# Moving one ScalarE copy and one set of V loads to other places in the instruction order of an attention and feed-forward kernel

## Chip, cores, metric

One core of one Trainium2 chip. The metric is the device time of one execution in microseconds (us), median of several runs.

## The reference

Batch 8, 8 heads, sequence S = 576, head dimension D = 64. Heads 0 to 3 use a local mask, heads 4 to 7 a strided one. The attention output, viewed as 4608 tokens of 512, goes through a feed-forward layer with a leaky activation.

```python
scores = scale * np.matmul(q, k.transpose(0, 1, 3, 2))
mask_local   = (rel >= 0) & (rel < 32)
mask_strided = (rel >= 0) & (pos[None, :] % 32 == pos[:, None] % 32)
# heads 0..3 local, heads 4..7 strided; masked softmax over the last axis
x = (attn @ v).transpose(0, 2, 1, 3).reshape(B * S, H * D)
h = x @ w_in                                    # 512 -> 2048
out = (np.maximum(h, 0) + alpha * np.minimum(h, 0)) @ w_out
```

## The kernel before

Two things run interleaved: the feed-forward matmuls of a chunk of 512 tokens (`lin1_piece`, line 570, and `lin2_piece`, line 611) and the attention of the batch after it, cut into small pieces that are fed in between. Attention works in pairs of heads, four pairs to a batch: pairs 0 and 1 are local, 2 and 3 strided. From batch 2 on, three of the four results are transposed by a DMA through the crossbar. The result of the first strided pair needs one more reordering: ScalarE copies it from the landing tile `xs` into `xT`, the input of the feed-forward layer (line 435). The fourth pair is transposed on TensorE (`x_piece`).

```python
pspool = ctx.enter_context(tc.tile_pool(name="ps", bufs=3, space=bass.MemoryType.PSUM))
# ...
def load_v(b, strided):                 # local V: one of two buffers, vls[b % 2]; issued by GpSimd, casts
    # ...
    keep(nc.gpsimd.dma_start(v16[r0:128, :, 0:64], ...))     # 3072 rows of 64 elements
# ...
def score_both(P):                      # the scores of a pair, in two halves
    # half 0: PSUM "sp"; exp (L366) and mask on GpSimd (L368) at once
    # half 1: two PSUM tiles of pool "ps"; its two exps (L372) are deferred by a piece each
    defer.extend([lambda: ex(0), lambda: ex(1)])
# ...
def x_piece(P):
    xp = pspool.tile([128, 1024], F16, tag="ps", name="xp")  # needs a "ps" buffer: freed by ex(0)
    for t in range(P.n):
        keep(nc.tensor.transpose(xp[...], P.x16[...], ident[...]))              # L413
    # ... keep(nc.scalar.copy(xT[...], xp[...]))                                 # L417

def x_dma(P):
    P.xs = xpool.tile([128, 8, 80], F16, tag="xs", bufs=2, name="xs")
    keep(nc.sync.dma_start_transpose(P.xs, P.x16[0:80, :]))                     # L428

def x_copy(P):
    keep(nc.scalar.copy(xT[:, P.hp, base : base + S]..., P.xs[:, :, 0:72]...))  # L435
```

For step g the pieces are: scores of pair g (S), the probability-times-V pieces of pair g-1 (P), the TensorE transposes of queries and keys (T), those of the result of pair g-2 (X). Each piece may carry loads and copies:

```python
def run(...):
    fn()
    # ... casts of V, q and k
    if lastp:
        if 4 * DX <= g - 1 < npair and pairs[g - 1].xd:
            x_dma(pairs[g - 1])
        if g % 4 == 0 and DX <= c < B:
            transpose_d()
        if g % 4 == 2 and DX <= c and c + 1 < B:
            load_d(c + 1)               # strided q and k of the next batch (qsd, ksd)
        if g % 4 == 2 and c + 2 < B:
            load_v(c + 2, False)        # local V, two batches ahead
    if copyp and 4 * DX <= g - 2 < npair and pairs[g - 2].xd and pairs[g - 2].strided:
        x_copy(pairs[g - 2])
```

Here c = g // 4 is the batch. For batch 2 the pairs are 8 to 11: V of batch 4 and q and k of batch 3 are loaded in step 10, the DMA of pair 10 is issued in step 11, its copy in the third piece of step 12, and the transposes of pair 11 come in step 13.

The softmax here doesn't subtract the row's maximum and nothing guards it: scores larger than these inputs give would overflow.

## Time and profile before

| | before |
|---|---|
| median | 328.12 us (3 runs, 328.0 to 329.12) |
| span of the profiled run | 326.4 us |
| TensorE busy | 314.9 us |
| TensorE idle | 11.5 us, of which one wait of 4.02 us |
| landing of the xs DMA after its issue | 2.6 us least, 2.7 median, 8.4 most |

A wait line reads: engine, tile and line that waited, "<-", what it waited for, then total us, times, longest. In the lines in order of time the columns are start, duration, engine, line, what; in brackets stands the idle time of that engine before it and what ended it. The lines themselves are shown in the prediction.

### The profile page before, as it was taken

The page shows a single profiled execution, that of the slowest core. Times are in us where ns is not written, and L with a number is a line of the kernel's source. Part 1 is how long each engine was busy: PE and PEld are TensorE (multiplying, and loading weights), DVE is VectorE, ACT ScalarE, POOL GpSimd, SP SyncE. Part 2 cuts the span into 40 slices and gives each one's busy share as a digit, 9 for nine tenths or more (in the row PEclk, how much of TensorE's full clock was granted, in tenths as well). Part 3 has the DMA queues.
Part 4 walks back from the last instruction along what each step waited for, and adds up shares of the span by engine and source line. Part 5 has one row for each costly group of instructions (what it writes and reads, how often), then busy time and mean ns, then how long its engine had stood idle before and what let it go on. Part 6 is the DMA issues. An engine that isn't in the chain of part 4 may idle for free.

```text
span 326.4 us, 6321 instructions
## 1 busy us (share of the span) xinstructions
PE 314.9 (96%) x2493; PEld 162.9 (50%) x2493; DVE 182.4 (56%) x356; ACT 173.1 (53%) x321; POOL 140.8 (43%) x152
## 2 busy tenths in 40 slices
PE   7999999999995999999999999999999999999995
PEld 3564455554552445444558754445544444444444
DVE  5576836488540884278427843784378328505801
ACT  2655655477335664576457735773566247415610
POOL 8832397308996362936293619351803300000000
PEclk9999999999997999999999999999999999999999
DMA  7999999996499798969987997371710230021011
GB/s 220 192 206 206 226 225 176 146 252 172 91 152 149 198 113 89 171 192 104 97 127 237 104 85 147 91 92 40 160 50 1 58 91 22 0 93 38 0 64 64
DMA packets 77597, 40.33 MB, mean 124 GB/s; under 512 B 58480, under 2 KB 69248, under 8 KB 77568
## 3 DMA queue, kind: packets, MB, share of 16 engines
q0 software_dynamic: 41728, 17.38, 49.2%
q1 hardware_dynamic: 35840, 22.55, 28.0%
q8 instruction: 19, 0.31, 0.4%
q14 instruction: 10, 0.08, 0.1%
HBM read 38.01 MB, written 9.44 MB: 145 GB/s over the span
## 4 chain that ended last, share of the span: by engine, by line
PE 85%; issue 4%; DMA 4%; DVE 2%; POOL 2%; ACT 1%; SPq 0%; POOLq 0%; ACTq 0%; DVEq 0%
PE hps L570 35%; PE ops L611 34%; PE pv L396 4%; DMA xs<-x16s 3%; PE tp L235 2%; PE wps L633 2%; DMA ql<-in_q_dram 2%; PE sp L353 1%; PE ops L603 1%; PE xp L413 1%; PE sp L311 1%; PE sph L311 1%; PE sph L353 1%; DVE x L405 1%; DVE qT L177 1%
## 5 line engine op out<-in xcount | busy, mean ns | idle before, releaser
L583 DVE SCALAR_TENSOR_TENSOR gT<-neg,oma,hps 128x512 f16<-128x512 f32 x144 | 106.2, 744 | 57.3 <-ACT neg L580 49.3
L611 PE MATMUL ops<-wout,gT 128*128 128x512 f16 x560 | 135.7, 380 | 0.0
L570 PE MATMUL hps<-xT,win 128*128 128x512 f16 (+1 forms) x640 | 134.0, 360 | 0.4
L580 ACT ACTIVATE neg<-hps 128x512 f32<-128x512 f32 x144 | 86.0, 597 | 40.1 <-PE hps L570 40.1
L570 PEld LDWEIGHTS <-win 128*128 128x128 f16 x640 | 60.6, 98 | 60.7 <-issue 5.3
L611 PEld LDWEIGHTS <-gT 128*128 128x128 f16 x560 | 49.2, 98 | 47.2
L368 POOL TENSOR_TENSOR et<-et,consts 128x576 f16<-128x576 f16 (+1 forms) x24 | 30.6, 1273 | 89.3 <-ACT et L366 89.2
L616 ACT COPY osb<-ops 128x512 f32<-128x512 f32 x35 | 20.5, 585 | 57.3 <-PE ops L611 53.3
L403 DVE RECIPROCAL rc<-pv 72x6 f32<-72x6 f32 (+2 forms) x80 | 14.9, 186 | 53.2 <-PE pv L396 52.7
L405 DVE TENSOR_TENSOR x<-pv,rc 96x384 f16<-96x384 f32 (+2 forms) x62 | 33.0, 532 | 2.1
L396 PEld LDWEIGHTS <-et 72*128 72x128 f16 (+1 forms) x448 | 24.1, 98 | 16.6 <-POOL et L375 0.9
L375 POOL TENSOR_TENSOR et<-et,consts 128x576 f16<-128x576 f16 (+1 forms) x24 | 30.5, 1270 | 0.2 <-POOL et L368 0.2
L366 ACT ACTIVATE et<-sp 128x576 f16<-128x576 f32 (+1 forms) x24 | 15.5, 646 | 10.6 <-PE sp L353 10.6
L372 ACT ACTIVATE et<-sph 128x288 f16<-128x288 f32 (+1 forms) x48 | 18.6, 409 | 0.0
L633 PE MATMUL wps<-wrm 128*128 128x512 f16 x44 | 16.4, 449 | 1.2 <-DVE wrm L645 1.2
L396 PE MATMUL pv<-vs,et 72*128 72x65 f16 x256 | 15.7, 193 | 0.0
L167 POOL DMA_DIRECT2D vl<-in_v_dram x8 | 11.1, 1390 | 9.5 <-PE pv L396 7.8
L179 POOL COPY vs<-stv 72x1024 f16<-72x1024 f16 x14 | 14.4, 1035 | 0.0
L177 DVE COPY qT<-tp 128x1024 f16<-128x1024 f16 (+1 forms) x10 | 10.1, 1008 | 4.1 <-PE tp L235 4.1
L353 PEld LDWEIGHTS <-kT 64*128 64x128 f16 x336 | 7.1, 95 | 9.9 <-issue 8.9
L435 ACT COPY xT<-xs 128x576 f16<-128x576 f16 x6 | 7.8, 1308 | 7.6 <-DMA xs<-x16s 7.6
L417 ACT COPY xT<-xp 128x576 f16<-128x576 f16 x10 | 6.4, 639 | 10.1 <-PE xp L413 10.1
(79 smaller groups left out, 201.6 us busy)
## 6 DMA issues: line engine op xcount, KB each, us to landing
out_dram<-osb SPq DMA_DIRECT2D x35, 256.0 KB, 2.3
ql<-in_q_dram SPq DMA_DIRECT2D x6, 512.0 KB, 4.8
kl<-in_k_dram SPq DMA_DIRECT2D x6, 512.0 KB, 5.4
stv<-in_v_dram POOLq DMA_DIRECT2D x8, 288.0 KB, 6.7
vl<-in_v_dram POOLq DMA_DIRECT2D x6, 384.0 KB, 10.1
win<-in_moe_w_in_dram POOLq DMA_DIRECT2D x4, 512.0 KB, 9.4
wout<-in_moe_w_out_dram POOLq DMA_DIRECT2D x4, 512.0 KB, 17.0
qsd<-in_q_dram POOLq DMA_DIRECT2D x6, 288.0 KB, 7.0
```

What stands on the lines that cost most here:

```text
L366: keep(nc.scalar.activation(ev.rearrange("r (y c) -> r y c", y=2), sp[0:r, :, 0:n], AF.Exp, scale=SCALE))
L368: keep(nc.gpsimd.tensor_tensor(mv, mv, m, op=ALU.mult))
L372: keep(nc.scalar.activation(ev[:, n * y : n * y + n], sps[y][0:r, 0:n], AF.Exp, scale=SCALE))
L375: keep(nc.gpsimd.tensor_tensor(mv, mv, m, op=ALU.mult))
L396: keep(nc.tensor.matmul(pv[:, 65 * x : 65 * x + 65], et[0:r, c : c + 128], v16[0:r, 2 * P.pr + hh, t, :] if P.strided else v16[:, 6 * (2 * ...
L405: keep(nc.vector.tensor_tensor(P.x16[0:w, c0 : c0 + 64 * nb].rearrange("r (c e) -> r c e", e=64), pvv[:, :, 0:64], rc[0:w, 0:nb].unsqueeze ...
L570: keep(nc.tensor.matmul(hps[:, dst : dst + w], win16[:, kk, 128 * m : 128 * m + 128], xT[:, kk, src : src + w], start=(kk == 0 and x == 0) ...
L580: keep(nc.scalar.activation(neg, hps, AF.Relu, scale=-1.0))
L583: keep(nc.vector.scalar_tensor_tensor(gTs[n][:, m, :], neg, oma[:, m : m + 1], hps, op0=ALU.mult, op1=ALU.add))
L611: keep(nc.tensor.matmul(ops, gTs[n][:, kf, 128 * mt : 128 * mt + 128], wout16[:, kf, :], start=(kf == 0), stop=(kf == 15)))
L616: keep(nc.scalar.copy(osb, ops))
L633: keep(nc.tensor.matmul(wps, wrm[:, 0:128], wrm, start=True, stop=True))
```

## The change

Its intent: a copy on ScalarE that waits for a DMA holds up what is behind it in ScalarE's queue (in the trace before, all of it ran only after the copy, from 100.50 us on). The copy is placed one step later, so that the DMA has landed by then, and the local V loads of batches 4 to 7, of which that of batch 4 was in flight together with this DMA, are issued three steps later (V of batch 4 in step 13 instead of 10).

```diff
-        copyP = min(2, len(seq) - 1)
...
-                    if g % 4 == 2 and c + 2 < B:
-                        load_v(c + 2, False)
-                if copyp and 4 * DX <= g - 2 < npair and pairs[g - 2].xd and pairs[g - 2].strided:
-                    x_copy(pairs[g - 2])
+                    if g % 4 == 1 and DX < c and c + 1 < B:
+                        load_v(c + 1, False)
+                if first and 4 * DX <= g - 3 < npair and pairs[g - 3].xd and pairs[g - 3].strided:
+                    x_copy(pairs[g - 3])
```

(`first` is the first piece of a step. The lines after it move up by one: L570, L611, L616 become L569, L610, L615.)

More of the change, by code (lines that the diff above doesn't have):

```diff
@@ L512, with run @@
                 extra = [todo.pop(0) for _ in range(min(cnt, len(todo)))]
-            def run(fn=fn, extra=extra, g=g, c=c, kind=kind, lastp=(i == lastP), copyp=(i == copyP)):
+            def run(fn=fn, extra=extra, g=g, c=c, kind=kind, lastp=(i == lastP), first=(i == 0)):
                 fn()
```

## The prediction

> **What bounds the kernel now.** I read the page's first parts, then the list of waits of TensorE, then the order of time around its one long wait, and last the chain of work that ended last. The page (row: engine, busy us, share, instructions; then tenths in 40 slices of 8.16 us):
>
> ```profile
> PE 314.9 (96%) x2493; PEld 162.9 (50%) x2493; DVE 182.4 (56%) x356; ACT 173.1 (53%) x321; POOL 140.8 (43%) x152
> ...
> PE   7999999999995999999999999999999999999995
> ...
> PEclk9999999999997999999999999999999999999999
> ```
>
> TensorE is the bound: 314.9 of 326.4 us busy, so only 11.5 us are idle, some 3 us each at the start and the end. One slice in the middle, the thirteenth (98 to 106 us), is different: busy 5 tenths, clock 7 tenths. The waits of TensorE, all of them over 1 us:
>
> ```profile
> PE xp L413 <- ACT et L372: 4.0, 1, 4.0
> PE wps L633 <- DVE wrm L645: 1.2, 1, 1.2
> ```
>
> So what can be won is one wait of 4 us, once. ScalarE in order of time there (start, duration, engine, line, what):
>
> ```profile
> 92.05 0.71 ACT L372 ACTIVATE et<-sph 128x288 f16<-128x288 f32 x2
> 99.30 1.30 ACT L435 COPY xT<-xs 128x576 f16<-128x576 f16 x1 [6.54 <-DMA xs<-x16s]
> 100.50 0.58 ACT L616 COPY osb<-ops 128x512 f32<-128x512 f32 x1
> 100.98 0.66 ACT L366 ACTIVATE et<-sp 128x576 f16<-128x576 f32 x1
> 101.52 0.71 ACT L372 ACTIVATE et<-sph 128x288 f16<-128x288 f32 x2
> ```
>
> The crossbar-result copy (L435) of batch 2 sits at the head of ScalarE's queue from 92.76 to 99.30. Behind it wait an output eviction and the exps of pair 13, the second of which (L372) frees the PSUM buffer that the transposes of pair 11 (xp, L413) need. Then TensorE:
>
> ```profile
> 96.94 1.03 PE L611 MATMUL ops<-wout,gT 128*128 128x512 f16 x4
> 101.99 0.42 PE L413 MATMUL xp<-consts,x 72*128 72x72 f16 x8 [4.02 <-ACT et L372]
> ```
>
> Why the DMA was late: the issue list shows xs<-x16s landing after 2.6/2.7/8.4 us (minimum, median, maximum). The 8.4 is this one, issued at 90.89. The GpSimd queue just before it:
>
> ```profile
> 86.88 0.78 POOL L121 DMA_DIRECT2D qsd<-in_q_dram  x1
> 87.66 0.71 POOL L121 DMA_DIRECT2D ksd<-in_k_dram  x1
> 88.35 1.47 POOL L167 DMA_DIRECT2D vl<-in_v_dram  x1
> ```
>
> These landed after 5.3, 7.0 and 11.6 us, at 92.2, 94.7 and 99.9. An output store issued at 90.16 (landed 97.6) also stands ahead of xs. xs landed at 99.3, with V.
>
> **What the Trainium skill says.** "Perfetto Trace Analysis", Tensor Engine Instruction, says that ACT is a strict FIFO; the trace agrees: the eviction and exps ran only after the copy, at 100.50 and later. "DMA: Bandwidth & Descriptors", Issuing engines are not separate DMA queues, says that transfers from any issuer run on the same 16 DMA engines and interleave; the trace agrees, 8.4 us against 2.7 with V beside it. "TensorE: Matmul & The Clock Gate", What's actually happening, says that an idle window of about 3.4 us drops the clock to half, until about as long a busy one; the trace agrees: after 4.02 us idle the granted clock is 0.50 at 104 to 106 us, and the page shows one such slice only.
>
> **The change, part by part.** No work is added or removed; per engine the instruction counts are the same (the order comparison has 242, 184, 156 and 67 rows on DVE, ACT, POOL and SP on both sides). Two things move.
>
> *What the wait costs now.* The steady stage gives the measure: xp starts 0.86 us after the last ops group before it (135.71 to 136.57), so here it was due at 96.94 + 0.86 = 97.80; it came at 101.99: 4.19 us lost. From xp to the next xp is 101.99 to 136.57 = 34.58 us in this stage and 136.57 to 169.47 = 32.90 in the next, the same work: 1.68 us, which I give to the half clock. Sum 5.87 us.
>
> *The copy, one step later.* In the new ScalarE order it comes after pair 13's first exp (L366) and before the two of L372, no longer before L366 and the eviction. xp is thus still behind the copy. From starts in the rows above: copy to next 1.20 (99.30 to 100.50), then exp 0.40, then 0.07 to TensorE: xp at copy start + 1.67. The copy can start at 96.46 at the earliest: scores of pair 13 at 95.52, exp 0.40 later (as 128.15 to 128.55), next instruction 0.54 later (100.98 to 101.52). With an unchanged landing at 99.30, xp would come at 100.97, and the move alone would win 1.0 us.
>
> *V a batch later.* V of batch 4 is no longer issued at 88.35 but in the next stage, after the q and k casts. A measure for the transposes without it is batch 6, where no V is loaded: q and k issued at 213.06 and 213.81 (k landed 6.4 later, 220.2), a transpose (xT<-x) issued at 215.60 landed 5.2 later, at 220.8, 0.6 after k. With V the same three transposes took 7.6 to 8.5. In batch 2, k would then land near 94.2; add 0.6, about 0.9 for the store ahead (256 KB at about 280 GB/s, the rate while it ran), and up to 1 for the small tail loads beside it: xs at 95.7 to 97.3, I take 96.8. Then xp is at 96.8 + 1.67 = 98.47, 0.67 late, far too short for the clock to drop. Gain here: 5.87 - 0.67 = 5.2 us.
>
> *Steady batches 3 to 6.* xs lands at about 130.7 and the copy would start at 134.55, so it waits for nothing; the next exp runs 135.75 to 136.15, and xp may start at 136.22, due at 136.57: 0.35 us to spare. Nothing won or lost. V's issue on GpSimd falls where it has idle time (5.6 us before 111.77), its buffer's last reader is a stage back, and the loads land more than 20 us before use.
>
> *Last batch, a cost.* Before, the copy ran at 264.15, ahead of the last xp. Now it is the last ScalarE work of the attention, after the copy L417 and right before the hps matmuls that read it (the third of the first group does):
>
> ```profile
> 266.64 0.64 ACT L417 COPY xT<-xp 128x576 f16<-128x576 f16 x1 [1.19 <-PE xp L413]
> 267.10 4.85 PEld L570 LDWEIGHTS <-win 128*128 128x128 f16 x23
> 267.31 4.91 PE L570 MATMUL hps<-xT,win 128*128 128x512 f16 x22
> ```
>
> Copy 266.64 + 0.54 = 267.18 to 268.49, TensorE 0.07 later at 268.56; the third matmul was due at 267.31 + 2 x 0.216 = 267.74. Loss 0.8 us.
>
> **Sum:** 5.2 - 0.8 = 4.4 us, so 328.12 - 4.4 = 323.7 us, 1.3% less.
>
> **Rivals.** (1) *xs stays late*: it was held by q, k and the store, not by V. For: the store did not land until 97.6 and nothing of the hardware queue moved from 88 to 92. Against: the q0 packets of 94 to 99 us are nearly all small, V's size, and batch 6 shows 5.2 against 8. Then only 1.0 to 2 us come from the wait, the half clock may partly stay, and the last batch takes 0.8: 326 to 327.5. (2) *All won, nothing paid*: xs lands before 96.4 and the last copy hides; 328.12 - 5.87 + 0.33 = 322.6, and not under 322.2 without both waits gone. That is 1.8%, still under 2%. (3) *V collides later*: issued in the next stage beside q and k loads of 512 KB and the transposes of q and k, needed by pair 14 soon after. Before they had 2.85 us to spare (landing 107.6, scores 110.45), and the stage now starts earlier while the transposes, too, are issued earlier. If it bites, 1 to 2 us at batch 3: 325. (4) *A stall in each batch* from the copy between two exps: 0.35 us of margin; if ScalarE runs an eviction in between, 0.3 x 4 = 1.2 us more.
>
> **Range and chances.** The largest term, 5.87, is measured; open are the landing (0.3 to 2 us) and rivals 3 and 4. Eight in ten: 322.4 to 325.7. Faster by over 2% needs under 321.6, more than the whole wait and clock loss: 0.04. Within 2%: 0.94. Slower by over 2% would need a new stall of over 10 us: 0.02.
>
> **What would show it.** In the changed profile: xs of batch 2 landing after about 6 us, not 8.4; the wait of xp for L372 under 1.2 us or gone from the list; the thirteenth slice at 9 in busy and clock; xp to xp of that stage 32.9; a new wait of hps for the L435 copy of about 0.8 us near 263; TensorE idle near 8 us. It is wrong if xs still lands with the clock low, if a wait of sp for the transposed k appears in the next stage, or if each batch shows a wait at xp.

## The result

| | before | after |
|---|---|---|
| median | 328.07 us (4 runs, 328.0 to 329.12) | 323.59 us (4 runs, 323.48 to 323.78) |
| span of the profiled run | 326.4 us | 321.7 us |
| TensorE idle in it | 11.5 us | 8.4 us |
| mean granted clock | 0.995 | 0.999 |

The ratio is 0.9845, 95% interval 0.9819 to 0.9871; the four runs listed on each side give 0.9863 by their medians and 0.9857 by their means, both inside that interval. The gain is clear of noise, and it is under 2%.

The page after, busy shares and slices:

```profile
PE 313.3 (97%) x2493; PEld 162.4 (51%) x2493; DVE 183.2 (57%) x356; ACT 172.8 (54%) x321; POOL 140.6 (44%) x152
...
PE   7999999999999999999999999999999999999995
...
PEclk9999999999999999999999999999999999999999
```

The thirteenth slice, 5 tenths busy at 7 tenths of the clock before, is now like its neighbours. The waits of TensorE after:

```profile
PE wps L632 <- DVE wrm L644: 1.2, 1, 1.2
PE hps L569 <- ACT xT L435: 0.6, 1, 0.6
...
PE xp L413 <- ACT et L372: 0.2, 1, 0.2
```

The 4.0 us wait has shrunk to 0.2, and one that was not there has come: hps waits for the copy L435. ScalarE in order of time around batch 2, after:

```profile
95.96 0.65 ACT L366 ACTIVATE et<-sp 128x576 f16<-128x576 f32 x1 [0.70 <-PE sp L353]
96.52 1.30 ACT L435 COPY xT<-xs 128x576 f16<-128x576 f16 x1
97.73 0.70 ACT L372 ACTIVATE et<-sph 128x288 f16<-128x288 f32 x2
```

The copy starts 0.56 us after the exp's start, which is that exp's own pace: it no longer waits for the DMA. That landed 5.6 us after its issue at 90.94, near 96.5, just in time. The landing times of the six xs DMAs, first before, then after, and the load of V that was at 88.35 before:

```profile
DMA to landing us min/median/max: 2.6/2.7/8.4
...
DMA to landing us min/median/max: 2.7/2.7/5.6
...
101.95 1.49 POOL L167 DMA_DIRECT2D vl<-in_v_dram  x1
```

The other end of the kernel, TensorE at the start of the last-but-one chunk:

```profile
260.95 1.03 PE L610 MATMUL ops<-wout,gT 128*128 128x512 f16 x4
261.15 0.64 ACT L417 COPY xT<-xp 128x576 f16<-128x576 f16 x1 [2.39 <-PE xp L413]
...
261.69 1.31 ACT L435 COPY xT<-xs 128x576 f16<-128x576 f16 x1
261.82 0.59 PE L569 MATMUL hps<-xT,win 128*128 128x512 f16 x2
...
263.05 3.18 PE L569 MATMUL hps<-xT,win 128*128 128x512 f16 x14 [0.64 <-ACT xT L435]
```

Two matmuls run, and the third, due 2 x 0.216 us after 261.82, at 262.25, starts at 263.05: 0.80 us lost.

The sum from the two traces. The scores of pair 13 stand at 95.52 before and at 95.56 after, so all up to there is equal, 0.04 us apart. The xp transposes come at 101.99 and 98.18: 3.85 us won, that offset taken out. From xp to the next xp it is 34.58 us before and 98.18 to 131.08 = 32.90 us after: 1.68 won. The last batch loses 0.80. Together 3.85 + 1.68 - 0.80 = 4.73 us; the spans differ by 4.7.

That the 1.68 us are the clock can be seen in the trace before, in stretches of 2 us (busy time and instruction count of TensorE, its weight loads, VectorE, ScalarE and GpSimd, then granted clock, DMA share, GB/s):

```profile
102.00:104.00 2.00, 2.00 (x14) 0.99 (x14) 0.00 (x0) 1.17 (x3) 2.00 (x3) 0.70 1.03 230
104.00:106.00 2.00, 2.00 (x7) 0.63 (x5) 0.00 (x1) 0.89 (x2) 2.00 (x2) 0.50 0.95 167
106.00:108.00 2.00, 2.00 (x15) 1.00 (x14) 1.39 (x2) 1.01 (x2) 0.19 (x1) 0.95 0.80 122
```

The missing shares of the clock, 0.30, 0.50 and 0.05 of 2 us each, come to 1.7 us. After the change the clock is 1.00 in all three.

### The profile page after: what moved, and what is told of

The parts are those of the page before. It is cut to its first block, busy times and chain, and to the rows that moved or that the text cites. A ratio compares the mean times of both kernels' runs of the same rounds, so it can differ in the third digit from the quotient of the medians.

```text
span 321.7 us, 6320 instructions
## 1 busy us (share of the span) xinstructions
PE 313.3 (97%) x2493; PEld 162.4 (51%) x2493; DVE 183.2 (57%) x356; ACT 172.8 (54%) x321; POOL 140.6 (44%) x152
## 4 chain that ended last, share of the span: by engine, by line
PE 86%; issue 5%; POOL 2%; DVE 2%; DMA 2%; ACT 2%; SPq 0%; POOLq 0%; ACTq 0%; DVEq 0%
PE ops L610 36%; PE hps L569 35%; PE pv L396 4%; DMA kl<-in_k_dram 2%; PE tp L235 2%; PE sp L353 2%; PE wps L632 1%; PE ops L602 1%; PE xp L413 1%; PE sph L311 1%; PE sp L311 1%; PE sph L353 1%; DVE x L405 1%; PE sp L295 1%; POOL vs L179 1%
## 5 line engine op out<-in xcount | busy, mean ns | idle before, releaser
L610 PE MATMUL ops<-wout,gT 128*128 128x512 f16 x560 | 135.3, 379 | 0.0
L569 PE MATMUL hps<-xT,win 128*128 128x512 f16 (+1 forms) x640 | 132.7, 358 | 1.1 <-ACT xT L435 0.6
L569 PEld LDWEIGHTS <-win 128*128 128x128 f16 x640 | 60.2, 98 | 60.2 <-issue 3.9
L610 PEld LDWEIGHTS <-gT 128*128 128x128 f16 x560 | 49.2, 97 | 47.2
L615 ACT COPY osb<-ops 128x512 f32<-128x512 f32 x35 | 20.5, 586 | 64.8 <-PE ops L610 64.5
L396 PE MATMUL pv<-vl,et 128*128 128x65 f16 x192 | 10.9, 194 | 0.4 <-POOL et L375 0.4
```

The costliest lines, as they stand in the source:

```text
L396: keep(nc.tensor.matmul(pv[:, 65 * x : 65 * x + 65], et[0:r, c : c + 128], v16[0:r, 2 * P.pr + hh, t, :] if P.strided else v16[:, 6 * (2 * ...
L569: keep(nc.tensor.matmul(hps[:, dst : dst + w], win16[:, kk, 128 * m : 128 * m + 128], xT[:, kk, src : src + w], start=(kk == 0 and x == 0) ...
L610: keep(nc.tensor.matmul(ops, gTs[n][:, kf, 128 * mt : 128 * mt + 128], wout16[:, kf, :], start=(kf == 0), stop=(kf == 15)))
L615: keep(nc.scalar.copy(osb, ops))
```

## The experiments

The theory of the prediction: V's packets hold the xs DMA up, that holds ScalarE's queue, that holds a PSUM buffer, TensorE idles and then runs at half clock for a while; the later copy gives little in batch 2 and costs as much in batch 7. The rivals: the place of the copy does it; or V's later place helps in every stage; or the time lost beside the wait is not the clock.

e1 to e4 ran in one set of rounds, e5 to e8 in a second, e9 and e10 in a third, each on another chip. The kernel before ran in all three, with medians of 329.02, 328.63 and 329.13 us, so across the sets a difference of some 0.5 us is not to be read from the medians alone.

### e1: the copy alone

```diff
 (on the changed kernel)
-                    if g % 4 == 1 and DX < c and c + 1 < B:
-                        load_v(c + 1, False)
+                    if g % 4 == 2 and c + 2 < B:
+                        load_v(c + 2, False)
```

> The copy one pair step later, V loaded when it was before. Theory V (the late V load is what helps batch 2): xs of batch 2 still lands after about 8.4 us, near 99.3, so xp comes at 99.3 + 1.67 = about 101.0, TensorE waits about 3 us there, the granted clock drops again for about 4 us or perhaps not (a wait of 3.0 against 4.0 us), and the last batch pays 0.8: 326.2 to 328.2 us. Rival C (the place of the copy in ScalarE's queue is what helps): most of the gain is here, 324.5 us or less.

Measured: median 327.86 us, ratio 0.9959 (0.9932 to 0.9985). The xs DMA landed after 8.8 us. The wait stood as before, shorter by 0.6 us:

```profile
PE xp L413 <- ACT et L372: 3.4, 1, 3.4
...
PE hps L569 <- ACT xT L435: 0.6, 1, 0.6
```

The six runs fall in two groups: five of 327.78 to 328.28 us with a mean clock of 0.995, and one of 325.78 us with a clock of 1.000. So the place of the copy is not what made the kernel faster: the five stand beside 328.14 to 328.29 us, the four runs of the kernel before in the same rounds that had that clock. (Its other seven had 0.987 to 0.990 and took 329.0 to 329.5 us; they and the lone run make up most of the ratio's distance from 1. A lower clock goes with a longer time there, but no trace of such a run was kept.) The mean of the five is 328.00, which is 2.2 us above the lone run. That is not the price of the half clock alone: the clock column of the profiled run comes to 1.7 us, and the lone run has no trace. Its wait was probably also the shorter one (see e8).

### e2: V alone

```diff
 (on the kernel before)
-                    if g % 4 == 2 and c + 2 < B:
-                        load_v(c + 2, False)
+                    if g % 4 == 1 and DX < c and c + 1 < B:
+                        load_v(c + 1, False)
```

> V a batch later, the copy where it was before. Theory V: xs lands near 96.5 as in the changed kernel; behind it come the copy (1.20), the eviction (0.48), the first exp (0.54) and the exp that frees the buffer (0.47), so xp at about 99.2, 1.35 us late instead of 0.34; clock full; no 0.8 us at the last batch. 328.1 - 5.9 + 1.35 = 323.6 us, the same as the whole change. Rival C: 326.5 us or more.

Measured: 323.75 us median (323.57 to 324.02), ratio 0.9845 (0.9826 to 0.9865). The copy starts when the DMA lands, at 96.86, and TensorE waits 1.5 us; the clock stays at 1.00; no wait at the last batch.

```profile
96.86 1.30 ACT L435 COPY xT<-xs 128x576 f16<-128x576 f16 x1 [3.98 <-DMA xs<-x16s]
98.07 0.58 ACT L616 COPY osb<-ops 128x512 f32<-128x512 f32 x1
98.54 0.66 ACT L366 ACTIVATE et<-sp 128x576 f16<-128x576 f32 x1
99.09 0.71 ACT L372 ACTIVATE et<-sph 128x288 f16<-128x288 f32 x2
```

This is the whole gain of the change without its first half: ScalarE still stands 4 us in front of the DMA, but what it holds back is needed only about 1.5 us earlier than it comes.

### e3: only V of batch 4

```diff
 (on the kernel before)
-                    if g % 4 == 2 and c + 2 < B:
+                    if g % 4 == 2 and DX < c and c + 2 < B:
                         load_v(c + 2, False)
+                    if g == 13:
+                        load_v(4, False)
```

> As e2, but only the V load of batch 4 is moved; those of batches 5 to 7 stay where they were before. If the collision in batch 2 is the whole of it, the same as e2 within 0.3 us (323.6). If the later V loads bring something in each stage too, it is slower than e2 by 0.5 us or more.

Measured: 323.61 us median (323.27 to 323.95), ratio 0.984 (0.982 to 0.986), the same as e2. The other three V loads may be early or late; only the one in step 10, which meets the xs DMA in step 11, matters. In the later stages the loads are issued some 12 us before the xs DMA (116.18 and 128.04 in the kernel before), and it lands after 2.7 us either way.

### e5: half of V

The kernel before, with each of these V loads cut into two of 12 row groups, the first where it was, the second a batch later.

> The kernel before, with each V load of batches 4 to 7 cut in two: half of the rows where it was, the other half a batch later. If V's packets in the DMA queues hold xs up, xs of batch 2 lands between the two, near 97.9 (about 7.0 us after its issue), and xp comes 2.7 us after that, near 100.6: 2.8 us late, the clock perhaps dropping: 325.0 (clock kept) to 327.2 (clock dropped). If it is all or nothing (any V load ahead holds xs to the end of q and k, or to 99.3), xs lands at 96.5 or at 99.3.

Measured: 326.61 us median, ratio 0.9921 (0.9891 to 0.9951). The xs DMA was issued at 90.8 and landed 6.9 us later, at 97.7: between 5.3 to 5.8 (no V: the change, e2, e3, e4, e7) and 8.1 to 8.8 (all of it: the kernel before, e1, e8), so the delay follows how much of V is in flight. Rows and bytes were halved together, so which of them counts stays open. TensorE waited 2.50 us, xp came at 100.39. Three runs had a clock of 0.995 (326.57 to 326.96 us), one of 1.000 (324.91). So a wait of 2.5 us already drops the clock in most runs, and it costs 326.72 - 324.91 = 1.8 us here. The profiled run, in stretches of 2 us as above:

```profile
98.00:100.00 2.00, 0.00 (x0) 0.00 (x0) 0.00 (x0) 2.00 (x4) 0.34 (x1) 1.00 0.24 24
100.00:102.00 2.00, 1.61 (x12) 0.79 (x12) 0.00 (x0) 1.27 (x4) 1.88 (x2) 0.64 1.05 205
102.00:104.00 2.00, 2.00 (x6) 0.73 (x5) 0.00 (x0) 0.59 (x1) 2.00 (x3) 0.50 1.01 224
104.00:106.00 2.00, 2.00 (x16) 1.01 (x15) 1.00 (x2) 1.22 (x3) 1.63 (x2) 1.00 0.94 154
```

TensorE is busy all through 102 to 104 us, but does 6 matmuls at a clock of 0.50: the busy share alone hides this loss, the clock column shows it (0.36 and 0.50 of 2 us missing, 1.7 us).

### e8: TensorE kept busy through the wait

e1, with 14 matmuls of no use ahead of the xp transposes of pair 11 (the lines that put `fill_x` in X's place in step 13, and V's load back as in e1, are left out).

```diff
+                def fill_x(g=g):
+                    t = pbpool.tile([128, 2, 512], F32, tag="sp", name="sp")
+                    for _ in range(14):
+                        keep(nc.tensor.matmul(t[:, 0], wrm[:, 0:128], wrm, start=True, stop=True))
+                    X(g - 2)()
```

> As e1 (copy later, V early), with 14 matmuls of 128x512 that compute nothing of use put ahead of xp of pair 11, into a PSUM buffer that is free then: 14 x 0.216 = 3.0 us of the 3.4 us in which TensorE idled. If the half clock after the wait costs about 2 us, the granted clock stays at 1.00 in all runs and the time is 325.8, as in the one run of e1 whose clock stayed up (325.78). If the lost time is something else, it stays near 328.

Measured: 326.42 us median of six runs, ratio 0.993 (0.9905 to 0.9955). The granted clock was 0.998 to 1.000 in every one of them. So keeping TensorE busy did keep the clock up, and the median is 1.4 us below that of e1, in other rounds. The time was not the 325.8 expected in all runs: they spread from 325.81 to 327.24. In the profiled run (326.09 us) xs landed after 8.1 us instead of 8.8, the exp that frees the buffer ended at about 100.66, the fillers at 100.82, and xp followed at once, so 0.5 us earlier than in e1 (101.33).

The traces part the two. From the start of this xp to the end of the span it is 222.7 us where the clock is kept and the last copy is early (e2, e3, e4, e7, e10), and 223.5 us where the clock is kept and the last copy is late (the change, e6, e8). It is 224.4 us in the kernel before and in e5, and 225.2 in e1: 1.7 us more in each of the three with the half clock, and in e8, which is e1 with fillers, not. By this measure the spans of e8's six runs (324.0 to 325.5 us) put their xp at 100.5 to 102.0, and that of the lone run of e1 (324.0 us) at 100.5; these are estimates. A landing of xs that differs from run to run would do it, but no trace of those runs was kept.

### e10: q and k sooner, V where it was

Is it V, or all that is in the software queue? The kernel before, with the strided q and k loads of batch 3 one step sooner.

```diff
-                    if g % 4 == 2 and DX <= c and c + 1 < B:
+                    if g % 4 == (1 if c == DX else 2) and DX <= c and c + 1 < B:
                         load_d(c + 1)
```

> The kernel before (V early, copy early), with the q and k loads of the strided heads of batch 3 issued 2.5 us sooner. Theory S (xs is held by all the software-queue loads in flight together, q, k and V): they end sooner, V lands near 97, xs near 96.5, xp 2.7 us after it, near 99.2, clock kept: 323.6 to 325 us although V has not been moved. Rival V (it is V alone, issued 2.5 us ahead of xs, that holds it): xs still lands after 8 us or more, the time stays within 0.5 us of the kernel before.

Measured: 324.99 us median (324.4 to 325.53), ratio 0.9876 (0.9859 to 0.9892). The xs DMA landed 5.1 us after its issue, which itself came at 92.2 instead of 90.9, because a new wait arose on the way, of the mask on GpSimd:

```profile
PE pv L396 <- POOL et L368: 1.2, 1, 1.2
PE xp L413 <- ACT et L372: 0.8, 1, 0.8
```

V has not been moved, and most of the gain is there: what held xs was the sum of the GpSimd-issued loads in flight with it (the "software queue", q0 in the page), not V as such. Four traces make the square: xs lands after 8.4 us with q, k and V beside it (the kernel before), 5.6 with q and k (the change), 5.1 with V (here), and 3.0 with none of them (e9). In the last two k still landed 0.6 to 1.1 us after xs was issued, and xs was issued 1.3 us later, which gave V more of a start here; that part is not separated. Of the two that were moved, V is the one that could go without a new wait.

### e6: q and k behind xs

The whole change, with these two loads issued in step 11 behind the xs DMA.

```diff
-                    if g % 4 == 2 and DX <= c and c + 1 < B:
+                    if g % 4 == (3 if c == DX else 2) and DX <= c and c + 1 < B:
                         load_d(c + 1)
```

> The whole change, and the q and k loads of the strided heads of batch 3 issued behind the xs transpose of batch 2 instead of 4 us ahead of it. If these two loads hold the rest of xs's delay (5.6 us against 2.7 elsewhere), xs lands within 3.0 to 4.2 us. The time stays 323.6 within 0.4 us, as the copy can't start before 96.5 anyway, unless the transposes of q and k now come late for pair 14.

Measured: 325.25 us median (324.92 to 325.51), ratio 0.9889 (0.9865 to 0.9914): a miss. The edit did not put the loads behind xs but around it: they were issued at 90.52 and 91.27, the xs DMA at 90.79, and it landed after 7.5 us, at 98.3; k landed at 99.1. Being in flight with it is enough to hold it. This run also settles a rival of the prediction, the 256 KB output store that is issued just ahead of xs on the same queue: elsewhere it was slow when xs was (7.4 us in the kernel before, 4.8 after the change), but here it landed after 2.2 us, near 92.3, and xs was still late. TensorE waited 2.1 us, and here the clock stayed at 1.00 in all four runs.

### e4: the whole change but for the last batch

```diff
+                if first and 4 * DX <= g - 3 < npair - 4 and pairs[g - 3].xd and pairs[g - 3].strided:
+                    x_copy(pairs[g - 3])
+                if copyp and g - 2 == npair - 2:
+                    x_copy(pairs[g - 2])
```

> The whole change, but the copy of the last batch stays where it was before. If that copy costs 0.8 us at the last batch as reckoned: 323.6 - 0.8 = 322.8 us, and the wait of hps for the copy is gone. If the 0.64 us wait hides elsewhere: 323.4 to 323.6.

Measured: 322.69 us median (322.59 to 323.06), ratio 0.9814 (0.9795 to 0.9834), and no wait of hps for L435. The median is 0.9 us below that of the change.

### e7: the copy behind the exp that frees the buffer

As e4, with the copy of batches 2 to 6 in the second piece of the step instead of the first (`first=(i == 1)`).

> As e4, but the copy of batches 2 to 6 is put one piece later, behind the exp that frees the buffer for xp (and ahead of the second one). xp of batch 2 then waits for nothing: the 0.34 us left there go, 322.3 to 322.4 us. If the copy now delays the next copy (L417) or the exp behind it, it is 322.7 or more.

Measured: 322.25 us median (322.21 to 322.29), ratio 0.9799 (0.9775 to 0.9822), the lowest median of all. It is 0.4 us below e4's, in other rounds; the trace bears it out, with a wait of xp of 0.36 us in e4 and none here. ScalarE and TensorE in batch 2:

```profile
96.48 0.41 ACT L372 ACTIVATE et<-sph 128x288 f16<-128x288 f32 x1
96.77 1.31 ACT L435 COPY xT<-xs 128x576 f16<-128x576 f16 x1
97.96 0.43 ACT L372 ACTIVATE et<-sph 128x288 f16<-128x288 f32 x1
```

```profile
96.95 1.03 PE L613 MATMUL ops<-wout,gT 128*128 128x512 f16 x4
97.81 0.42 PE L413 MATMUL xp<-consts,x 72*128 72x72 f16 x8
```

xp now follows its ops group by 0.86 us, as in an undisturbed stage. The copy stands between the two exps of the second half, behind the one that TensorE needs.

### e9: e7 with q and k sooner

> As e7 (V later, the copy behind the first exp, the last copy early), with the q and k loads of the strided heads of batch 3 issued 2.5 us sooner. If these loads hold the rest of xs's delay, xs lands in 3 to 4 us instead of 5.6. No wait on TensorE is left there, so the time stays 322.3 within 0.3 us: a transfer that lands earlier than it is needed brings nothing.

Measured: 323.71 us median (323.55 to 323.9), ratio 0.9836 (0.9823 to 0.985). The first half came as expected: no xs DMA took longer than 3.0 us to land, so q and k do hold the rest of its delay. The time did not stay: it is 1.5 us above e7. The two loads take GpSimd 0.78 and 0.71 us to issue, and stood ahead of the mask of pair 10, which GpSimd reached late already:

```profile
83.44 1.03 POOL L179 CAST kl<-kl 128x1024 f16<-128x1024 f32 x1
84.42 0.78 POOL L121 DMA_DIRECT2D qsd<-in_q_dram  x1
85.19 0.71 POOL L121 DMA_DIRECT2D ksd<-in_k_dram  x1
85.92 1.29 POOL L368 TENSOR_TENSOR et<-et,consts 72x576 f16<-72x576 f16 x1
87.16 1.28 POOL L375 TENSOR_TENSOR et<-et,consts 72x576 f16<-72x576 f16 x1
```

TensorE's first pv of pair 10 waited 1.16 us for that mask, to 87.27, and xp came at 99.13 instead of 97.81, 1.3 us later. Another 0.19 us went in a new wait of pair 14's scores for the transposed k. A landing that nobody waited for was bought with a wait on the path.

## Why the prediction was right

- **The bound and the one wait to be won.** Right: in the changed kernel nothing else on TensorE moved beyond 0.1 us up to pair 13, and the whole difference lies in that wait, the clock after it, and the last batch.
- **What the wait costs, 5.87 us.** Right as a sum (3.85 won + 0.34 left in the wait, 1.68 at half clock). The clock term was given to the clock by argument only; the clock columns of the kernel before, e1 and e5 come to 1.7 us each, their traces are 1.7 us longer behind xp, and e8 shows that filling the wait keeps the clock up.
- **The copy alone wins 1.0 us in batch 2.** Right in kind: e1's wait is 3.4 instead of 4.0 us, 0.6, with xs landing 0.4 us later than in the trace before. With the 0.8 us of the last batch it is nothing.
- **V later: xs lands between 95.7 and 97.3.** It landed near 96.5, in the range, but the working has a slip: k at 87.66 + 6.4 = 94.1, plus 0.6, 0.9 and up to 1, gives 95.6 to 96.6, so neither 97.3 nor the 96.8 taken comes out of its terms. That is why xp came at 98.18 and not at 98.47, and it is the 0.3 us between the 4.4 us forecast and the 4.7 measured. That the sum of the terms fits does not show each of them: e6 speaks against the one for the store. The cause was put a little too narrowly: e10 shows that it is the sum of the software-queue loads, of which V is the last.
- **Steady batches win and lose nothing.** Right: xp to xp is 32.90 us, no wait at xp.
- **The last batch costs 0.8 us.** Right: 0.80 us in the trace, and e4 without it is 0.9 us faster in the median.
- **Rivals.** Rival 1 (xs stays late) fell: 5.6 us. In part it was right all the same, as q and k hold the rest of the delay (e9: 3.0 us without them); the store does not (e6). Rival 3 (V collides later) fell: transposed q and k took 6.9 and 6.8 us to land, but no scores waited for them. The room was 0.9 us (k landed near 104.05, scores at 104.96), where it had been 2.85. Rival 4 fell. Rival 2's figure of 322.6 is what e4 came to (322.69), as it leaves the change's own cost out.
- **What the prediction did not say** is that V alone would do: it worked out the copy alone, but not V alone, and e2 has the same time as both together. Of the two halves of the change, one is the gain, and the other is worth 1.3 us in batch 2 (a wait of 1.5 us in e2 against 0.2) and costs 0.8 us in batch 7 when it is applied there too. That e2 and the change still come out 0.2 us apart is within their spread.

## What to carry to other kernels

Before moving an instruction in an in-order queue, ask what the queue behind it holds and when that is needed: e2 left ScalarE standing 4 us, which cost TensorE only 1.5, and e7 took away the last wait by placing the copy behind the one exp that frees a buffer. The DMA on the critical path was cleared here by moving bulk loads out of its flight. V a batch later brought no new wait in batch 2, q and k moved to about the same time (e6) held it again, and loads moved ahead (e10, e9) their issue time on GpSimd cost a wait. Look at the last iteration by itself: a move that is free in the steady state can land right before its consumer there.

## What the Trainium skill lacked or had wrong

- "TensorE: Matmul & The Clock Gate", Why this matters for your kernels, advises no idle gaps over about 3 us. Here a gap of 2.5 us dropped the clock in three of four runs (e5), one of 3.4 us in five of six (e1), and one of 2.1 us in none of four (e6); each gap is that of the one profiled run, the other runs are told by their mean clock. The loss, in the three traces that show it, was 1.7 us on top of the gap.
- "DMA: Bandwidth & Descriptors", Issuing engines are not separate DMA queues, says that transfers of all issuers interleave, which holds; neither it nor the rest of the page has a figure for a small crossbar transpose beside bulk loads. Here one that lands after 2.6 to 3.0 us without them took 5.1 to 8.8 us beside GpSimd-issued loads of q, k and V, whether they were issued before it (5.3 to 5.8 us beside q and k, 6.9 with half of V, 8.1 to 8.8 with all of it) or at the same time (7.5 us, e6).
- The same section calls the time to initiate a DMA "usually small relative to the DMA itself". That is true here too (1.49 us for V against 9.9 to landing, after the change), but on GpSimd it is time in the queue of its compute work: two issues of 0.78 and 0.71 us ahead of a mask cost TensorE a wait of 1.16 us (e9).
